# One prefix-product scan over a chunk's four head pairs in place of four, with its factors kept in a tile of their own

## The chip, the cores and the metric

The kernel runs on one core of a Trainium2 chip. The metric is the device time of one execution in microseconds (us). Five engines run their own in-order instruction streams: PE (matrix multiply, with PEld for its weight loads), DVE (elementwise and scans), ACT (activation functions), POOL, and SP, which here only issues transfers. They wait for one another by semaphores.

## The reference, cut to what matters

The program is a gated linear attention, then a two-layer expansion with a squared ReLU, then a soft mixture of experts:

```python
f = 1.0 / (1.0 + np.exp(-f_logit))                      # B=4, H=8, S=768, D=48
for t in range(S):
    state = f[:, :, t, :, None] * state + k_t (outer) v_t
    y[:, :, t] = q_t @ state
x = y as tokens x (heads * D)                           # 3072 x 384
h = np.maximum(x @ w_in, 0.0); x = (h * h) @ w_out      # d_ff = 2048
# then a soft MoE: 8 experts of 4 slots, F = 1024
```

The recurrence is computed by chunks with inverse prefix products: `ip[t]` is the product of `1 + exp(-f_logit)` (that is `1/f`) up to `t`, clamped from above at 1e15. Keys are multiplied by `ip`, queries by `1/ip`, and what remains inside a chunk is a masked matrix product.

## The kernel before, in words

**Attention.** The 3072 tokens are 24 chunks of 128 (`C`), six (`CB`) to a batch row. Eight heads make four pairs (`NP`); a pair lies on 112 partitions (`DD`: head 0 on 0 to 47, head 1 on 64 to 111). `prep(i)` makes a chunk's operands in stages. In the first stage ACT takes `exp(-f)` in place in the chunk's load slot (L154); 1 is added in place, on ACT for the chunks 2, 3 and 4 (`ONACT`, L156) and on DVE for the others (L158); and DVE runs one scan per pair (L160), `state = min(f[t] * state, 1e15)`, whose second operand is one column `big` repeated along 128 elements. A scan begins from 1.0 in a batch row's first chunk (`first`) and otherwise from the last column of the previous chunk's `ip`, read as one value per partition. Chunk 0 is done in two halves of two pairs. In the second stage ACT takes `exp(-ln(ip))` (L167, L168), and DVE makes `kt = k * ip` (L169). In the third stage DVE refines the inverse by a Newton step in a tile `t` with one buffer (L175, L176) and makes `qt = q * -(1/ip)` (L177).

`chunk(i)` is the matrix work: transposes of `kt` (L191) copied by ACT (`n`, L193), scores (L203) masked by DVE (`a`, L206), state updates (L218, added by DVE on L226), and values (L241, L248), which ACT and DVE bring into `y` (L252, L257). `y` is then sent into the token matrix `x` by six small transfers (L263, L266). All transfers are issued by SP in one order: `y` out, the loads of later chunks (`g<-fkq` L134, `v` L136) and the weight loads (`raw<-w` L303). A chunk's `f`, `k` and `q` lie in one of three slots, so a load waits until the last reader (L177) of the chunk three before it is done.

**The expansion.** The tokens are six blocks of 512. For each of the 16 column groups of the hidden layer (`ff`), `layer1` is nine matmuls of 512 columns (L116 to L118, split-precision in three parts), ACT makes `r` and `gh` (L343, L345, L346), DVE makes the remainder `gl` (L348), and `layer2` is nine more matmuls, of which those of L118 need `gl`. Each weight group is loaded raw (L303) and split once: ACT L313, L317 and L111, DVE L318, L319, L327 and L112. A block of `x` is split into two parts (L111 on ACT, L112 on DVE) before its first `layer1`.

**Order.** The program is written as an interleaving (`stream`, `upto`, `target`), and a scheduler that models durations orders each engine's ready instructions, so that neighbours on DVE come from different chunks and from the weight splits. Matrix work of the expansion begins after 23 attention steps (`FIRST`).

Of the kernel before, what the change touches and what calls it, by code (L numbers as in the profile page):

```python
# [7 lines left out]
F32 = mybir.dt.float32  # L8
# [3 lines left out]
AF = mybir.ActivationFunctionType  # L12
ALU = mybir.AluOpType
# [4 lines left out]
NP = H // 2  # L18
HR = 64
DD = HR + D  # L20
TB = 512
NB = B * S // TB
C = 128
# [25 lines left out]
PLACE[6] = [(0, 32, 0, 96), (32, 16, 2, 96)]  # L49
PLACE[7] = [(0, 32, 1, 96), (32, 16, 2, 112)]  # L50
BIG = 1e15
FAR = 1.875 * 2.0**-96
LEAST, MOST = 1.125 * 2.0**-15, 2.0**16 * (1.875 - 2.0**-20)


class K:
# [12 lines left out]

    def consts(self, cp):  # L70
        nc, A = self.nc, self.A
        self.big = cp.tile([DD, 1], F32, name="big")
        nc.vector.memset(self.big, BIG)
        nc.scalar.preload_act_table_set("natural_log_exp_and_others")
        self.mask = cp.tile([128, HC], F32, name="mask")
        self.ident = cp.tile([128, 128], F32, name="ident")
        self.gd = cp.tile([DD, B * NP], F32, name="gd")
        self.ph = cp.tile([128, KT, NS], F32, name="ph")
        self.m = cp.tile([NC * NS, 1], F32, name="m")
        self.wsum = cp.tile([128, NFF], F32, name="wsum")  # L80
        if A["w"].dtype == F32:
            nc.vector.memset(self.wsum, 0.0)
        self.s = cp.tile([NC * NS, 1], F32, name="s")
        self.alpha = cp.tile([NC * NS, 1], F32, name="alpha")
        self.SI = cp.tile([NC * NS, DM], F32, name="SI")
        self.ct = [cp.tile([128, TB], F32R, name=f"ct{b}") for b in range(NB)]
        self.fold = cp.tile([128, 128 + NC], F32, name="fold")
# [11 lines left out]
    def attention_state(self, ap):  # L99

        self.sums = [ap.tile([DD, NP * D + HR - D], F32, name=f"S{j}") for j in range(4)]
        self.turn = 0
        for t in self.sums:
            self.nc.gpsimd.memset(t, 0.0)
# [37 lines left out]
    def prep(self, i):  # L142

        nc, ap = self.nc, self.ap
        U = self.U[i] = {}
        f, k, q, v = self.loaded.pop(i)
        first = i % CB == 0

        parts = [slice(0, NP // 2), slice(NP // 2, NP)] if i == 0 else [slice(0, NP)]
        ip = ap.tile([DD, NP, C], F32, tag="ip", name="ip", bufs=2)  # L150
        kt, qt = (ap.tile([DD, NP, C], F32, tag=n, name=n, bufs=3) for n in ("k", "q"))
        big = self.big.to_broadcast([DD, C])
        for s in parts:
            nc.scalar.activation(f[:, s], f[:, s], AF.Exp, scale=-1.0)  # L154
            if i in ONACT:
                nc.scalar.activation(f[:, s], f[:, s], AF.Copy, bias=1.0)  # L156
            else:
                nc.vector.tensor_scalar(f[:, s], f[:, s], 1.0, None, ALU.add)  # L158
            for p in range(s.start, s.stop):
                nc.vector.tensor_tensor_scan(ip[:, p], f[:, p], big, 1.0 if first else self.ip[:, p, C - 1 : C], ALU.mult, ALU.min)  # L160
        self.ip = ip
        if i % CB == CB - 1:
            bt = i // CB
            nc.vector.tensor_copy(self.gd[:, bt * NP : (bt + 1) * NP], ip[:, :, C - 1])
        yield
        for s in parts:
            nc.scalar.activation(f[:, s], ip[:, s], AF.Ln)  # L167
            nc.scalar.activation(f[:, s], f[:, s], AF.Exp, scale=-1.0)  # L168
            nc.vector.tensor_tensor(kt[:, s], k[:, s], ip[:, s], ALU.mult)  # L169
        U["k"] = kt  # L170
        yield

        t = ap.tile([DD, NP, C], F32, tag="t", name="t", bufs=1)
        for s in parts:
            nc.vector.tensor_tensor(t[:, s], ip[:, s], f[:, s], ALU.mult)  # L175
            nc.vector.scalar_tensor_tensor(t[:, s], t[:, s], 2.0, f[:, s], ALU.subtract, ALU.mult)  # L176
            nc.vector.tensor_tensor(qt[:, s], q[:, s], t[:, s], ALU.mult)  # L177
        yield
        U["v"], U["q"] = v, qt
        yield  # L180
# [604 lines left out]
    def out_of_range(self, pool):  # L785
        nc = self.nc
        bad = pool.tile([128, 1], F32, name="bad")
        nc.vector.tensor_reduce(bad, self.wsum, AX.X, ALU.max)
        nc.vector.tensor_scalar(bad, bad, FAR, None, ALU.is_ge)
        d = pool.tile([DD, 1], F32, name="d")  # L790
        nc.vector.tensor_reduce(d, self.gd, AX.X, ALU.max)
        nc.vector.scalar_tensor_tensor(bad[:DD], d, BIG, bad[:DD], ALU.is_ge, ALU.max)
        row = self.psm()[:1, :128]
# [152 lines left out]
```

## Time and profile before

| what | value |
|---|---|
| median of three runs | 609.6 us (606.76 to 612.16) |
| profiled execution, whole | 605.44 us |
| its span (first to last recorded instruction) | 603.6 us |
| PE busy | 573.8 us (95%) |
| DVE busy | 331.9 us (55%) |
| ACT busy | 316.4 us (52%) |
| mean granted TensorE clock | 0.994 |

The shares are averages over stages that differ: DVE is busy nearly all the time in the first 150 us and about a third of it after 300 us. PE's busy time includes waits inside its pipeline, so a busy PE is not a PE at its peak. The profiled execution is 4.2 us (0.7%) shorter than the median of the runs.

### The profile page before, as it was taken

How to read it: one execution, taken by the hardware profiler on the slowest of the kernel's cores; microseconds unless marked ns; L12 is line 12 of the kernel's file. 1: busy time of each engine (PE TensorE's matmuls, PEld its weight loads, DVE VectorE, ACT ScalarE, POOL GpSimd, SP SyncE). 2: the span in 40 equal slices, each digit the busy share in tenths (PEclk: the TensorE clock that was granted, in tenths of full speed). 3: DMA queues.
4: the chain of work that ended last, by engine and by line, in shares of the span. 5: the costliest groups of instructions: out<-in, count | busy, mean ns of one | idle time of the engine just before them, and what ended most of it. 6: DMA issues, size and time to landing. Idle time of an engine off the chain costs nothing.

```text
span 603.6 us, 13370 instructions
## 1 busy us (share of the span) xinstructions
PE 573.8 (95%) x5611; PEld 447.6 (74%) x5611; DVE 331.9 (55%) x695; ACT 316.4 (52%) x578; POOL 4.0 (1%) x10
## 2 busy tenths in 40 slices
PE   4899989999999999999999999999999999999993
PEld 3786757877777878768778778887788887886372
DVE  6999998999735467455464562542332332213322
ACT  5658778986545456354465353544343544543122
POOL 0000000000000000000000000000000100000000
PEclk9999998999999999999999999999999999999998
DMA  9657778413212202202211211220000735555657
GB/s 292 179 154 200 224 193 309 134 32 82 70 32 68 59 16 73 59 16 73 64 35 50 73 34 46 79 79 3 15 14 3 272 110 168 194 193 174 267 202 272
DMA packets 28324, 69.59 MB, mean 115 GB/s; under 512 B 4464, under 2 KB 17008, under 8 KB 28256
## 3 DMA queue, kind: packets, MB, share of 16 engines
q1 hardware_dynamic: 28256, 68.65, 36.0%
q8 instruction: 46, 0.75, 0.5%
q14 instruction: 22, 0.18, 0.1%
HBM read 59.20 MB, written 4.72 MB: 106 GB/s over the span
## 4 chain that ended last, share of the span: by engine, by line
PE 73%; DVE 9%; DMA 7%; ACT 6%; issue 2%; SPq 1%; ACTq 0%; DVEq 0%
PE o L116 10%; PE ph L116 10%; PE ph L118 9%; PE ph L117 9%; PE o L118 9%; PE o L117 9%; DMA g<-fkq 5%; PE psm L241 3%; DVE ip L160 2%; PE hp L560 2%; PE so L584 2%; PE psm L203 2%; PE psm L218 2%; DMA raw<-w 1%; PE psm L248 1%
## 5 line engine op out<-in xcount | busy, mean ns | idle before, releaser
L348 DVE TENSOR_TENSOR gl<-r,gh 128x512 fp32r<-128x512 f32 x96 | 66.2, 690 | 122.3 <-ACT r L346 121.8
L116 PE MATMUL ph<-x,w 128*128 128x512 f32 x288 | 118.0, 410 | 3.5 <-ACT x L111 2.1
L343 ACT ACTIVATE r<-ph 128x512 f32<-128x512 f32 x96 | 56.9, 593 | 121.5 <-PE ph L118 117.9
L116 PE MATMUL o<-gh,w 128*128 128x512 f32 x288 | 118.0, 410 | 0.0
L118 PE MATMUL ph<-x,w 128*128 128x512 f32 x288 | 113.7, 396 | 0.0
L117 PE MATMUL ph<-x,w 128*128 128x512 f32 x288 | 113.7, 395 | 0.0
L117 PE MATMUL o<-gh,w 128*128 128x512 f32 x288 | 113.1, 393 | 0.0
L118 PE MATMUL o<-gl,w 128*128 128x512 f32 x288 | 111.0, 396 | 1.1 <-DVE gl L348 1.0
L116 PEld LDWEIGHTS ph<-x,w 128*128 128x128 f32 x288 | 54.8, 190 | 19.4 <-issue 4.3
L118 PEld LDWEIGHTS o<-gl,w 128*128 128x128 f32 x288 | 54.0, 188 | 16.3 <-DVE gl L348 5.0
L118 PEld LDWEIGHTS ph<-x,w 128*128 128x128 f32 x288 | 54.5, 190 | 11.9 <-DVE x L112 0.2
L116 PEld LDWEIGHTS o<-gh,w 128*128 128x128 f32 x288 | 54.0, 187 | 12.5
L117 PEld LDWEIGHTS ph<-x,w 128*128 128x128 f32 x288 | 54.9, 191 | 10.9 <-DVE w L112 0.7
L345 ACT ACTIVATE gh<-r 128x512 fp32r<-128x512 f32 x96 | 60.8, 633 | 2.2
L346 ACT ACTIVATE r<-r 128x512 f32<-128x512 f32 x96 | 60.5, 630 | 1.9
L117 PEld LDWEIGHTS o<-gh,w 128*128 128x128 f32 x288 | 54.1, 188 | 9.9
L154 ACT ACTIVATE g<-g 112x512 f32<-112x512 f32 (+1 forms) x25 | 15.2, 611 | 40.2 <-DMA g<-fkq 40.2
L241 PEld LDWEIGHTS psm<-q,S 48*48 48x48 f32 (+1 forms) x704 | 26.5, 143 | 10.4 <-issue 5.6
L160 DVE TENSOR_TENSOR_SCAN ip<-g,ip,big 112x128 f32<-112x128 f32 x80 | 33.8, 469 | 0.6 <-ACT g L156 0.2
L241 PE MATMUL psm<-q,S 48*48 48x64 f32 (+1 forms) x704 | 31.0, 240 | 2.2 <-DVE S L224 1.3
L167 ACT ACTIVATE g<-ip 112x512 f32<-112x512 f32 (+1 forms) x25 | 15.3, 613 | 27.9 <-DVE ip L160 27.7
L177 DVE TENSOR_TENSOR q<-g,t 112x512 f32<-112x512 f32 (+1 forms) x25 | 16.5, 664 | 21.8 <-PE psm L241 21.7
(134 smaller groups left out, 647.1 us busy)
## 6 DMA issues: line engine op xcount, KB each, us to landing
m<-m SPq DMA_DIRECT2D x26, 768.0 KB, 4.3
g<-fkq SPq DMA_DIRECT2D x23, 672.0 KB, 5.3
raw<-w SPq DMA_DIRECT2D x16, 768.0 KB, 5.9
v<-v SPq DMA_DIRECT2D x24, 192.0 KB, 2.9
g<-m SPq DMA_DIRECT2D x6, 768.0 KB, 4.9
out_dram<-ob SPq DMA_DIRECT2D x18, 256.0 KB, 3.4
x<-y SPq DMA_DIRECT2D x48, 72.0 KB, 2.9
x<-y SPq DMA_DIRECT2D x48, 16.0 KB, 1.8
```

The costliest lines, as they stand in the source:

```text
L116: mm(out=out, lhsT=sh, rhs=mh, start=start, stop=False)
L117: mm(out=out, lhsT=sl, rhs=mh, start=False, stop=False)
L118: mm(out=out, lhsT=sh, rhs=ml, start=False, stop=stop)
L154: nc.scalar.activation(f[:, s], f[:, s], AF.Exp, scale=-1.0)
L160: nc.vector.tensor_tensor_scan(ip[:, p], f[:, p], big, 1.0 if first else self.ip[:, p, C - 1 : C], ALU.mult, ALU.min)
L167: nc.scalar.activation(f[:, s], ip[:, s], AF.Ln)
L177: nc.vector.tensor_tensor(qt[:, s], q[:, s], t[:, s], ALU.mult)
L241: nc.tensor.matmul(out=pz[h * HR : h * HR + m, p, r], lhsT=U["S"][c][d, p * D : p * D + m], rhs=U["q"][d, p, r], start=True, stop=True)
L343: nc.scalar.activation(r, o, AF.Relu)
L345: nc.scalar.activation(gh, r, AF.Square)
L346: nc.scalar.activation(r, r, AF.Square)
L348: nc.vector.tensor_tensor(gl, r, gh.bitcast(F32), ALU.subtract)
```

## The change

`consts` loses the column `big`. `attention_state` gets two tiles of 112 x 4 x 129, written once by DVE memsets: `fe` (factors, all 1e20) and `bound` (all 1e15). Column 0 of each pair is the extra one. Per chunk, column 0 of `bound` is set to 1.0 (a batch row's first chunk) or copied from the last column of the previous `ip`; `1 + exp(-f)` is written to columns 1 to 128 of `fe` and no longer in place; and one scan runs over the four pairs laid end to end, 516 elements. At a pair's column 0 the state is multiplied by 1e20 and cut to `bound`, which is the product so far, so the scan restarts there by itself. `ip` becomes a view with a pitch of 129 elements that begins at column 1. The tile `t` is gone: the Newton step writes its values over the factors in `fe`, of which there is one buffer.

```diff
+OVER = 1e20
@@ consts
-        self.big = cp.tile([DD, 1], F32, name="big")
-        nc.vector.memset(self.big, BIG)
@@ attention_state
+        self.fe, self.bound = (ap.tile([DD, NP, C + 1], F32, name=n) for n in ("fe", "bound"))
+        self.nc.vector.memset(self.fe, OVER)
+        self.nc.vector.memset(self.bound, BIG)
@@ prep
-        ip = ap.tile([DD, NP, C], F32, tag="ip", name="ip", bufs=2)
+        ipc = ap.tile([DD, NP, C + 1], F32, tag="ip", name="ip", bufs=2)
+        ip = ipc[:, :, 1:]
+        flat = lambda t, s: t[:, s].rearrange("d p t -> d (p t)")
+        fe, bound = self.fe, self.bound
+        if first:
+            nc.vector.memset(bound[:, :, 0], 1.0)
+        else:
+            nc.vector.tensor_copy(bound[:, :, 0], self.ip[:, :, C - 1])
-        big = self.big.to_broadcast([DD, C])
         for s in parts:
             nc.scalar.activation(f[:, s], f[:, s], AF.Exp, scale=-1.0)
             if i in ONACT:
-                nc.scalar.activation(f[:, s], f[:, s], AF.Copy, bias=1.0)
+                nc.scalar.activation(fe[:, s, 1:], f[:, s], AF.Copy, bias=1.0)
             else:
-                nc.vector.tensor_scalar(f[:, s], f[:, s], 1.0, None, ALU.add)
-            for p in range(s.start, s.stop):
-                nc.vector.tensor_tensor_scan(ip[:, p], f[:, p], big, 1.0 if first else self.ip[:, p, C - 1 : C], ALU.mult, ALU.min)
+                nc.vector.tensor_scalar(fe[:, s, 1:], f[:, s], 1.0, None, ALU.add)
+            nc.vector.tensor_tensor_scan(flat(ipc, s), flat(fe, s), flat(bound, s), 1.0, ALU.mult, ALU.min)
@@ prep, third stage
-        t = ap.tile([DD, NP, C], F32, tag="t", name="t", bufs=1)
+        t = fe[:, :, 1:]
```

## Rows read from the trace of the kernel before

**Rows 1.** Stretches: length, then busy us (instructions) by engine, granted clock, DMA share, GB/s.

```profile
15.00:85.00 70.00, 65.23 (x990) 51.63 (x989) 66.09 (x135) 47.78 (x85) 0.00 (x0) 1.00 0.67 196
85.00:90.00 5.00, 3.06 (x46) 2.00 (x44) 4.60 (x8) 4.01 (x9) 0.00 (x0) 1.00 0.47 99
90.00:95.00 5.00, 4.86 (x17) 3.22 (x18) 5.00 (x8) 3.78 (x7) 0.00 (x0) 0.66 1.00 357
98.00:150.00 52.00, 52.00 (x342) 41.99 (x342) 51.84 (x92) 44.22 (x78) 0.00 (x0) 1.00 0.34 109
98.00:500.00 402.00, 399.67 (x3605) 317.01 (x3605) 215.85 (x441) 216.54 (x397) 2.85 (x2) 1.00 0.22 67
```

**Rows 2.** The chain that ended last, up to 110 us: start, us, what.

```profile
44.54 6.91 DMA g<-fkq
...
63.33 1.52 DVE ip L160 x4
...
78.11 8.66 DMA raw<-w
```

**Rows 3.** The scans, line L160: the first 83 us, then from 98 us on.

```profile
L160 DVE TENSOR_TENSOR_SCAN ip<-g,ip,big x28: 455/462/487, 10.5 to 72.6; 112x128 f32<-112x128 f32 x28
L160 DVE TENSOR_TENSOR_SCAN ip<-g,big x8: 396/406/425, 4.2 to 56.9; 112x128 f32<-112x128 f32 x8
...
L160 DVE TENSOR_TENSOR_SCAN ip<-g,ip,big x52: 457/468/485, 101.6 to 348.3; 112x128 f32<-112x128 f32 x52
L160 DVE TENSOR_TENSOR_SCAN ip<-g,big x8: 400/415/426, 144.2 to 236.9; 112x128 f32<-112x128 f32 x8
```

**Rows 4.** DVE in order of time: start, us, line, what, count [idle before].

```profile
3.86 0.29 DVE L158 TENSOR_SCALAR g<-g 112x256 f32<-112x256 f32 x1 [3.00 <-ACT g L154]
...
10.49 1.60 DVE L160 TENSOR_TENSOR_SCAN ip<-g,ip,big 112x128 f32<-112x128 f32 x4
12.01 0.33 DVE L224 COPY S<-psm 112x192 f32<-112x192 f32 x1
...
47.28 0.16 DVE L164 COPY gd<-ip 112x4 f32<-112x4 f32 x1
47.36 0.69 DVE L169 TENSOR_TENSOR k<-g,ip 112x512 f32<-112x512 f32 x1
...
55.31 0.73 DVE L160 TENSOR_TENSOR_SCAN ip<-g,big 112x128 f32<-112x128 f32 x2
55.96 0.73 DVE L206 TENSOR_TENSOR a<-psm,mask 128x256 f32<-128x256 f32 x2
...
59.91 0.68 DVE L175 TENSOR_TENSOR t<-ip,g 112x512 f32<-112x512 f32 x1
60.51 0.95 DVE L112 TENSOR_TENSOR w<-whi,w 128x768 fp32r<-128x768 f32 x1
```

**Rows 5.** All engines in order of time, around the ACT additions of the chunks 2 and 3.

```profile
13.71 0.61 ACT L156 ACTIVATE g<-g 112x512 f32<-112x512 f32 x1
...
14.23 0.36 ACT L252 ACTIVATE y<-psm 112x256 f32<-112x256 f32 x1
...
15.82 0.67 DVE L177 TENSOR_TENSOR q<-g,t 112x512 f32<-112x512 f32 x1
...
22.12 0.69 DVE L177 TENSOR_TENSOR q<-g,t 112x512 f32<-112x512 f32 x1
22.33 0.63 ACT L156 ACTIVATE g<-g 112x512 f32<-112x512 f32 x1
```

**Rows 6.** PE in order of time, where the second block of tokens begins.

```profile
87.68 0.38 PE L218 MATMUL psm<-v,n 64*48 64x48 f32 x6
90.14 0.50 PE L116 MATMUL ph<-x,w 128*128 128x512 f32 x1 [2.09 <-ACT x L111]
```

**Rows 7.** All engines in order of time, one remainder `gl` and the matmuls that read it.

```profile
103.25 0.68 DVE L348 TENSOR_TENSOR gl<-r,gh 128x512 fp32r<-128x512 f32 x1
...
104.43 0.84 PE L118 MATMUL o<-gl,w 128*128 128x512 f32 x3
```

## The prediction, made before the result was known

> **What bounds the kernel now.** I began with the page's busy shares, but they average over stages, so the view that decides is busy time by stretch [rows 1]. From 98 to 500 us PE is busy for 399.67 of 402 us: whatever DVE does there, only 2.3 us of PE's idle time can be given back. From 15 to 85 us it is DVE that is full, 66.09 of 70 us (94%), while PE's figure of 65.23 us hides short waits between small matmuls. So a shorter DVE instruction can pay only ahead of 98 us, and it pays by letting PE enter its full stretch earlier. Second, the chain of waits [rows 2]: in that early part it goes through scans (63.33 us) but also through transfers of 6.91 and 8.66 us, which no DVE instruction shortens; they move only because SP issues them after a `y` that DVE finished. Third, the scans themselves [rows 3]: 28 + 8 lie in the first 83 us, that is nine chunks (0 to 8), and 52 + 8 after 98 us, fifteen chunks. Fourth, DVE in order of time [rows 4], from which I take prices as distances between starts, because neighbouring instructions overlap: an instruction listed at 0.69 us delays the next by less.
>
> **The scan.** Four scans with an initial value per partition hold DVE from 10.49 to 12.01 us, 1.52 us [rows 4]. Two that begin from the constant hold it from 55.31 to 55.96, 0.65 us, so four take 1.30 us. The long scan of 516 elements stands nowhere in this trace. From above: if a scan's cost were all per element, 0.325 us per 128 makes 1.31 us for 516. From below: an elementwise instruction of 512 delays its neighbour by 60.51 - 59.91 = 0.60 us, and a scan is not likely to be cheaper, so 0.60 us. Between them I need the fixed part of a scan, and take the nearest row of a tiny instruction: the copy of 112x4 at 47.28 delays its successor by 0.08 us. Then an element costs (0.325 - 0.08) / 128 = 1.91 ns and the long scan 0.08 + 516 x 1.91 ns = 1.07 us. I take 1.07.
>
> [...]
>
> **What is added per chunk.** The copy (or the memset to 1.0) of 112x4: 0.08 us as that row, at most the row's whole 0.16 us if the scan must wait for it to finish. So a chunk that is not first saves 1.52 - 1.07 - 0.08 = 0.37 us of DVE, with bounds of 1.52 - 1.31 - 0.16 = 0.05 and 1.52 - 0.60 - 0.08 = 0.84. A first chunk saves 1.30 - 1.07 - 0.08 = 0.15 us (-0.17 to 0.62); chunk 0, in two scans of 258, saves 1.30 - 2 x (0.08 + 258 x 1.91 ns) = 0.15 us as well. Over the nine early chunks: 7 x 0.37 + 2 x 0.15 = 2.9 us; bounds 7 x 0.05 - 2 x 0.17 = 0.0 and 7 x 0.84 + 2 x 0.62 = 7.1 us.
>
> **The two memsets at the start** (112x516 each) cost nothing: DVE sits idle for 3.00 us before its first real instruction at 3.86 us, waiting for ACT and the first load [rows 4]. Even at the elementwise 0.60 us each they are over long before. Without that cover they would add 1.2 us once. The dropped memset of `big` was in the same idle time.
>
> **The factors in one buffer.** `fe` holds the factors of chunk i + 1 and the Newton values of chunk i, so adding 1 for the next chunk waits for L177 of the last. Where DVE adds, this is only DVE's own order: the scan can no longer fill a hole between L175 and L177, but DVE is full anyway. Where ACT adds (chunks 2, 3, 4) it is a new wait across engines, and ACT's stream stands behind it. Chunk 2: L156 ran at 13.71 us, while L177 of chunk 1 ended at 15.82 + 0.67 = 16.49 [rows 5]. Held in place it would hold L252 (14.23 us) and with it the first `y`. The scheduler orders by readiness, so I expect L156 behind those, and the loss is small: chunk 1's scan and Newton step, no longer interrupted by two scans of chunk 2, end about 1 us earlier, and chunk 2's one scan starts later but is shorter. Chunk 3: L156 at 22.33 us against an end of L177 at 22.12 + 0.69 = 22.81: 0.5 us later. I charge 0.5 us, with 0 below, and above it 2.8 + 0.5 = 3.3 us, if L156 of chunk 2 keeps its place.
>
> **The views with a pitch of 129.** L169, L175, L176 and L177 now read or write `ip` and `t` in four runs of 128 at a pitch of 129, L158 writes so. No row of before has an odd pitch. Below nothing is gained; above, the saving of 0.37 us is gone when each of the four grows by 0.09 of its 0.60 us. I take no cost, since the runs stay 128 long and the element counts do not change.
>
> [...]
>
> **The sum.** 2.9 us of DVE time, of which 94% is in a full engine, 2.7 us; less 0.5 us for chunk 3's wait: 2.2 us. After 98 us the same saving of 15 chunks meets a PE that is full, and I count nothing. The profiled execution would go from 605.44 to 603.2 us; that execution is 4.2 us under the median of the runs, and against the median of 609.6 the forecast is 607.4 us. That is 0.4%, less than the 1% that a measurement of this kernel can tell from no change.
>
> **Rivals.**
>
> *It pays nothing (609.6 us).* Either the path ahead of 98 us is set by SP's order and the transfers of 6.91 and 8.66 us, so that DVE's time is taken up by waiting, or the elementwise instructions on odd starts eat the 0.37 us (each 0.09 longer, as above). For the first: transfers make the two longest pieces of the chain there. Against it: DVE is 94% busy, so few of its waits are for transfers.
>
> [...]
>
> *A long scan in front of `gl` (612.6 us, up to 617.8).* From 98 to 150 us DVE is full too, 51.84 of 52 us [rows 1]. There the scans stood singly or in pairs between other work, so that a `gl` waited at most 0.38 us for one. A long scan can't be parted: it holds DVE 1.07 us, 0.69 us longer. `gl` at 103.25 us ended at 103.93, its matmuls began at 104.43, a slack of 0.50 us [rows 7]. Where the scheduler puts a long scan ahead of a ready `gl`, PE loses up to 0.69 us once per chunk: fifteen chunks make 10.4 us at most, half of that 5.2. With the early gain that is 609.6 - 2.2 + 5.2 = 612.6, at most 609.6 - 2.2 + 10.4 = 617.8. It decides from 2.2 / 0.69, some three full hits, on; slower by over 1% takes twelve of fifteen. For it: DVE is in order and full. Against: after 150 us it is not, and the slack covers most of a hit.
>
> **How the numbers follow.** Forecast (607.4) 0.48; nothing 0.22; more than its length 0.16; a long scan before `gl` 0.14. The forecast's own range, from 0.0 and 7.1 us of DVE time and the 0 to 3.3 us on ACT, and from runs that spread over 606.76 to 612.16, is 604 to 611. With half of the third case and most of the fourth the range is 602.5 to 613.5. Faster by over 1% (under 603.5) takes nearly all of the third case or the upper bound of the scan: 0.14. Slower by over 1% (over 615.7) takes nearly the whole of the last one, or the chunk 2 wait in its worst place together with odd starts: 0.06. Within 1%: 0.80.
>
> **What would show it.** In the profile after: one scan per chunk, about 1.07 us from its start to the next instruction's (0.60 or 1.31 would show the step wrong); a tiny copy ahead of it at 0.08; L169 to L177 still at 0.68 to 0.69 us each (0.77 and more would show odd starts); L156 of chunk 2 behind L252; PE's gap of 2.09 us before the second block some 2 us earlier, and the stretch from there on as long as before. The forecast is wrong if the gap does not move, or if matmuls of L118 wait for `gl` more than before.

## The result, and the profile after

The change makes the kernel slower by a small amount: a median of 611.8 us (609.72 to 618.68, 20 runs) against 608.05 us of the kernel before beside it (605.88 to 612.16, 20 runs), a ratio of 1.0065 with an interval of 1.0045 to 1.0084, or +3.9 us by the ratio (the two medians are 3.7 us apart). The forecast was -2.2 us. The result lies within 1% either way, but the sign is wrong, and it is measured.

The profiled execution of the changed kernel takes 613.65 us with a span of 611.9 us, 8.3 us more than that of before. The two are further apart than the medians: before's profile lies 2.6 us under its median, the other 1.9 us above. So I read from them where time goes, and take from the medians how much.

In the code after, the scan is L169, the copy of the bound L161, ACT's addition L166, DVE's L168, and what was L169, L175, L176, L177 is L178, L184, L185, L186; L116 to L118 are L120 to L122, L252 and L255 are L261 and L264, L193 is L202.

Busy time by stretch of the kernel after, columns as in [rows 1]:

```profile
15.00:85.00 70.00, 62.77 (x938) 50.01 (x940) 61.95 (x117) 45.26 (x82) 0.00 (x0) 1.00 0.59 173
85.00:95.00 10.00, 5.72 (x105) 4.30 (x101) 8.12 (x13) 6.76 (x12) 0.00 (x0) 0.92 0.87 280
95.00:100.00 5.00, 4.65 (x11) 3.68 (x12) 4.67 (x7) 3.43 (x6) 0.00 (x0) 0.50 0.91 299
98.00:150.00 52.00, 51.61 (x307) 39.06 (x306) 48.26 (x80) 42.65 (x76) 0.00 (x0) 0.98 0.41 131
```

From 15 to 85 us DVE is now busy 61.95 of 70 us where it was 66.09, and it got through 117 instructions for 135. Four scans became one, so fewer were due; but PE too did only 938 of its 990. DVE did not get done sooner, it waited more. The low clock behind the second block's start is still there, later and longer: 0.50, the lower of the two levels in the clock records of both traces (1.00 and 0.50), from 95 to 100 us costs 5 x 0.50 = 2.5 us, where before lost 5 x 0.34 = 1.7 us [rows 1]; the 0.92 of the ten us ahead of it falls for the most part where PE is idle anyway (93.72 to 95.35 us). (The 1.00 of the first stretch does not hold for all of it; the last section says why.)

DVE in order of time in the kernel after (start, us, line, what, count [idle before]), a chunk's scan and what stands around it:

```profile
0.91 0.49 DVE L104 MEMSET fe<- 112x516 f32 x1 [0.91 <-PEq L948]
1.45 0.49 DVE L105 MEMSET bound<- 112x516 f32 x1
...
4.00 0.30 DVE L168 TENSOR_SCALAR fe<-g 112x256 f32<-112x256 f32 x1 [1.93 <-ACT g L164]
4.33 0.69 DVE L169 TENSOR_TENSOR_SCAN ip<-fe,bound 112x258 f32<-112x258 f32 x1
4.94 0.27 DVE L168 TENSOR_SCALAR fe<-g 112x256 f32<-112x256 f32 x1
...
12.99 0.17 DVE L161 COPY bound<-ip 112x4 f32<-112x4 f32 x1
13.06 0.35 DVE L235 TENSOR_TENSOR S<-S,psm 112x192 f32<-112x192 f32 x1
...
17.04 1.23 DVE L169 TENSOR_TENSOR_SCAN ip<-fe,bound 112x516 f32<-112x516 f32 x1 [0.92 <-ACT fe L166]
...
26.18 1.23 DVE L169 TENSOR_TENSOR_SCAN ip<-fe,bound 112x516 f32<-112x516 f32 x1
27.32 0.40 DVE L215 TENSOR_TENSOR a<-psm,mask 128x256 f32<-128x256 f32 x1
27.63 0.68 DVE L178 TENSOR_TENSOR k<-g,ip 112x512 f32<-112x512 f32 x1
...
34.72 0.96 DVE L116 TENSOR_TENSOR w<-whi,w 128x768 fp32r<-128x768 f32 x1 [1.41 <-ACT w L115]
...
36.26 1.23 DVE L169 TENSOR_TENSOR_SCAN ip<-fe,bound 112x516 f32<-112x516 f32 x1
```

The long scan holds DVE from 26.18 to 27.32 us, 1.14 us; the copy takes 0.07 us to its successor; the memsets end at 1.94 us, ahead of an idle time that still lasts 1.93 us. But chunk 2's scan starts behind 0.92 us of idling, chunk 3's stands at 26.18 us and chunk 4's at 36.26 us. Before, they stood at 22.99 and 32.13 us. This is the same view of the kernel before, where chunk 2's scans run in pieces between chunk 1's Newton steps, with chunks 3 and 4 behind:

```profile
14.44 0.48 DVE L160 TENSOR_TENSOR_SCAN ip<-g,ip,big 112x128 f32<-112x128 f32 x1
14.84 0.67 DVE L176 SCALAR_TENSOR_TENSOR t<-t,g 112x512 f32<-112x512 f32 x1
15.42 0.48 DVE L160 TENSOR_TENSOR_SCAN ip<-g,ip,big 112x128 f32<-112x128 f32 x1
...
22.99 1.61 DVE L160 TENSOR_TENSOR_SCAN ip<-g,ip,big 112x128 f32<-112x128 f32 x4 [0.18 <-ACT g L156]
...
32.13 1.61 DVE L160 TENSOR_TENSOR_SCAN ip<-g,ip,big 112x128 f32<-112x128 f32 x4
```

PE in order of time in the kernel after, first where the first block's 512-column matmuls begin and then where the second block's do:

```profile
49.71 0.80 PE L120 MATMUL ph<-x,w 128*128 128x512 f32 x1 [1.21 <-ACT x L115]
...
92.97 0.75 PE L227 MATMUL psm<-v,n 64*64 64x48 f32 x16 [2.69 <-ACT n L202]
95.35 0.79 PE L120 MATMUL ph<-x,w 128*128 128x512 f32 x1 [1.63 <-ACT x L115]
```

The gap of [rows 6] is not gone and not earlier: the second block's first such matmul moved from 90.14 to 95.35 us.

For all that follows I use five marks of a trace: when the first 512-column matmul starts (A), the 91st (B, where the second block begins), the 169th (C), the 265th (D), and when the last one of the two feed-forward layers starts (E); last, what remains of the span. Times in us, one execution each.

| kernel | A | B | C | D | E | rest |
|---|---|---|---|---|---|---|
| before | 46.70 | 90.14 | 111.00 | 135.21 | 552.35 | 51.25 |
| after | 49.71 | 95.35 | 119.52 | 143.95 | 558.76 | 53.14 |

The 3.0 us lost at A have become 8.5 us at C: 2.2 us are added between A and B and 3.3 between B and C, and some 2.6 of these 5.5 us are clock (2.5 - 1.7 = 0.8 us behind B, some 1.8 us between A and B; last section). From C to E both take about the same, 441.4 and 439.2 us: what was lost ahead of about 120 us is all that is lost there. Another 1.9 us lie behind E and have to do with the clock (last section).

### The profile page after: what moved, and what is told of

The parts are those of the page before. It is cut to its first block, busy times and chain, and to the rows that moved or that the text cites. A ratio compares the mean times of both kernels' runs of the same rounds, so it can differ in the third digit from the quotient of the medians.

```text
span 611.9 us, 13335 instructions
## 1 busy us (share of the span) xinstructions
PE 577.1 (94%) x5611; PEld 449.4 (73%) x5611; DVE 329.2 (54%) x649; ACT 318.3 (52%) x578; POOL 4.0 (1%) x10
## 4 chain that ended last, share of the span: by engine, by line
PE 81%; DMA 5%; DVE 5%; ACT 4%; SPq 2%; issue 2%; ACTq 0%; DVEq 0%
PE ph L120 11%; PE o L120 11%; PE ph L121 10%; PE ph L122 10%; PE o L122 10%; PE o L121 10%; PE psm L250 3%; DMA g<-fkq 3%; DMA raw<-w 2%; PE hp L569 2%; PE psm L212 2%; PE so L593 2%; PE psm L227 2%; PE psm L257 2%; PE psm L393 1%
## 5 line engine op out<-in xcount | busy, mean ns | idle before, releaser
L120 PE MATMUL ph<-x,w 128*128 128x512 f32 x288 | 119.4, 415 | 3.0 <-ACT x L115 2.8
L120 PE MATMUL o<-gh,w 128*128 128x512 f32 x288 | 118.2, 410 | 0.0
L121 PE MATMUL ph<-x,w 128*128 128x512 f32 x288 | 115.1, 400 | 0.0
L122 PE MATMUL ph<-x,w 128*128 128x512 f32 x288 | 114.5, 399 | 0.0
L122 PE MATMUL o<-gl,w 128*128 128x512 f32 x288 | 110.6, 395 | 0.6 <-DVE gl L357 0.5
L120 PEld LDWEIGHTS ph<-x,w 128*128 128x128 f32 x288 | 55.5, 193 | 19.6 <-issue 4.1
L122 PEld LDWEIGHTS ph<-x,w 128*128 128x128 f32 x288 | 55.2, 192 | 12.3
L122 PEld LDWEIGHTS o<-gl,w 128*128 128x128 f32 x288 | 53.7, 188 | 13.9 <-DVE gl L357 2.4
L120 PEld LDWEIGHTS o<-gh,w 128*128 128x128 f32 x288 | 54.0, 187 | 13.1 <-ACT gh L354 0.2
L121 PEld LDWEIGHTS ph<-x,w 128*128 128x128 f32 x288 | 55.6, 193 | 10.6
L186 DVE TENSOR_TENSOR q<-g,fe 112x512 f32<-112x512 f32 (+1 forms) x25 | 16.6, 667 | 26.5 <-PE psm L250 26.4
L169 DVE TENSOR_TENSOR_SCAN ip<-fe,bound 112x516 f32<-112x516 f32 (+1 forms) x25 | 29.6, 1184 | 1.1 <-ACT fe L166 0.9
L176 ACT ACTIVATE g<-ip 112x512 f32<-112x512 f32 (+1 forms) x25 | 15.4, 617 | 28.2 <-DVE ip L169 28.1
L227 PEld LDWEIGHTS psm<-v,n 64*64 64x64 f32 (+1 forms) x704 | 20.7, 145 | 12.1 <-issue 5.9
```

The lines of the kernel that those rows point to most:

```text
L120: mm(out=out, lhsT=sh, rhs=mh, start=start, stop=False)
L121: mm(out=out, lhsT=sl, rhs=mh, start=False, stop=False)
L122: mm(out=out, lhsT=sh, rhs=ml, start=False, stop=stop)
L169: nc.vector.tensor_tensor_scan(flat(ipc, s), flat(fe, s), flat(bound, s), 1.0, ALU.mult, ALU.min)
L227: nc.tensor.matmul(out=pu[c][m, p], lhsT=U["n"][r, p, m], rhs=U["v"][r, hd * D : hd * D + D], start=True, stop=True)
```

## First runs: the shared tile, the loads and the long scan, one at a time

Two other things than the scan had changed in the trace. The factor tile is shared by two chunks, so that ACT's addition for chunk 2 stands behind chunk 1's Newton step. And SP issues chunk 3's load later (SP's DMA issues in order of time, before and then after):

```profile
8.66 0.33 SPq L134 DMA_DIRECT2D g<-fkq  x1
17.63 1.39 SPq L263 DMA_DIRECT2D x<-y  x2
```

```profile
15.60 1.47 SPq L272 DMA_DIRECT2D x<-y  x2
17.12 2.50 SPq L275 DMA_DIRECT2D x<-y  x4
19.66 0.58 SPq L138 DMA_DIRECT2D g<-fkq  x1
```

The first theories were therefore: the single tile costs the time (W), the later load does (L), or the scan that can't be parted does (S). Each got runs.

**e1.** The changed kernel with the Newton step in `q`'s tile.

```diff
-        t = fe[:, :, 1:]
+        t = qt
```

> The changed kernel, but the Newton step works in the chunk's query tile (three buffers) and no longer in the factors' tile; the long scan stays. In its instruction stream SP still issues the load of chunk 3 behind the first y, as in the changed kernel. Theory W (the single factor tile: adding 1 for the next chunk waits for L186 of this one): the wait is gone, 0.31 us per early chunk remain gained, about 606 us, 2 to 3 us under the kernel before, and the first 512-column matmul back at 47 us or sooner. Theory L (the load of chunk 3 issued 11 us later): no change to the changed kernel, 611 to 612 us. Theory S (a long scan can't be parted): 611 to 612 us.

607.0 us, ratio 0.9981 (0.9953 to 1.0008). A is 45.36 us. The loss is gone, with the long scan still in: near what W expected, and against S. It is against L too: SP issues chunk 3's load at 19.46 us here, as late as in the changed kernel.

**e2.** The kernel before with the loads of chunks 3 and 4 issued behind the transfers of `y`.

```diff
+                self.sent = nc.sync.dma_start(out=xl[o : o + n, kt, ts], in_=y[h * HR + e : h * HR + e + n, KT])
...
-                        self.loaded[new] = self.chunk_load(new)
+                        with self.tc.issue_after(self.sent.ins) if new in (3, 4) else ExitStack():
+                            self.loaded[new] = self.chunk_load(new)
```

> The kernel before, with the loads of the chunks 3 and 4 made to follow the six transfers of the y before them on SP, as the changed kernel has it. Theory L: 611 to 612 us, the whole loss of 3.9 us, with the first 512-column matmul near 50 us. Theory W and theory S: 608 us, as the kernel before, since neither the tile nor the scan is changed.

610.2 us, ratio 1.0050 (1.0023 to 1.0077): most of the loss, with none of the change in it.

**e3.** The kernel before, its four scans kept, but the factors written to the tile of the Newton step.

```diff
+        fe = ap.tile([DD, NP, C], F32, tag="t", name="t", bufs=1)
...
-                nc.vector.tensor_scalar(f[:, s], f[:, s], 1.0, None, ALU.add)
+                nc.vector.tensor_scalar(fe[:, s], f[:, s], 1.0, None, ALU.add)
...
-        t = ap.tile([DD, NP, C], F32, tag="t", name="t", bufs=1)
+        t = fe
```

> The kernel before with its four scans, but 1 + exp(-f) is written into the tile t (one buffer) and the Newton step overwrites it there, as the changed kernel does in fe. The load of chunk 3 falls behind the first y here too. Theory W: the loss without the scan's gain, about 3.9 + 2.8 = 6.7 us, 614 to 615 us. Theory L: 611 to 612 us or somewhat more. Theory S: 608 us, since no scan is long.

608.9 us, ratio 1.0016 (0.9999 to 1.0034): about half of the loss at most, with the tile shared and chunk 3's load at 19.44 us. W and L both expected 611 us or more; S, which e1 contradicts, expected 608.

**e4.** The changed kernel with the loads of chunks 3 and 4 issued earlier in the program.

```diff
-                    if j == (4 if i < 2 else 1) and i != 2 and new < NCH:
+                    if j == (0 if i < 2 else 1) and i != 2 and new < NCH:
```

> The changed kernel, with the loads of the chunks 3 and 4 written earlier in the program, so that SP issues the load of chunk 3 ahead of the first y, as in the kernel before. Theory L: 606 to 608 us. Theory W: 611 to 612 us, because the factor tile is still one. Theory S: 611 to 612 us.

604.4 us, ratio 0.9948 (0.9928 to 0.9969). This is faster than both kernels, and faster than any of the theories expected: the change, long scan, shared tile and all, with two loads placed elsewhere.

So far e2 and e4 spoke for L, e1 and e3 against it. The next four crossed the three edits.

**e5.** The same edit of the loads in the kernel before.

> The kernel before, with the same early place of the loads of the chunks 3 and 4 in the program as in the changed kernel with early loads; the load of chunk 3 was ahead of the first y here already, that of chunk 4 moves ahead of the second. If the scan made the gain of 3.1 us in the changed kernel with early loads (theory L: the order of the loads had hidden it), this is 607 to 608 us, as the kernel before. If the edit of the loads itself is what is fast, whatever the scan (rival), this is 604 to 605 us as well.

607.3 us, ratio 0.9978 (0.9953 to 1.0004): the first of its two cases.

**e6.** e1 and e4 together.

> The changed kernel with both repairs: Newton step in the query tile and early loads. If the single factor tile costs something by itself once the loads are early (theory W beside L), 602 to 603 us, 1 to 2 us under the changed kernel with early loads alone. If the tile costs only by way of the late load (theory L alone), 604 to 605 us, the same as with early loads alone.

607.9 us, ratio 0.9990 (0.9967 to 1.0013), neither of its two cases. Taking the shared tile out of e4 does not gain, it loses: against W.

**e7.** e3 with the loads early.

> The kernel before with four scans, the factors and the Newton step in one tile of one buffer, and early loads. Against the changed kernel with early loads (604.4 us) it lacks only the long scan. If the scan's 0.31 us per early chunk is what was gained (2.8 us), 607 us. If the scan's length brings nothing by itself, 604 to 605 us.

611.3 us, ratio 1.0054 (1.0028 to 1.0080), neither of its two cases. The early loads, which gained in e4, go with a loss here: against L.

**e8.** e4 with chunk 3's load early and chunk 4's where it was.

> The changed kernel, with the load of chunk 3 alone written early; that of chunk 4 keeps its late place. Theory L, if it is the load of chunk 3 that counts: 604 to 606 us. If the load of chunk 4 made the gain: 610 to 612 us, as the changed kernel.

610.3 us, ratio 1.0035 (1.0009 to 1.0061): the second of its two cases, as if chunk 4's load had made e4's gain. But e7 loses with both loads early.

Every single theory is contradicted: the same edit gains in one company and loses in another. What all these kernels have in common is that any edit changes the order in which the four instruction streams are laid down when the program is built, everywhere in the first 110 us. That became the next theory (O).

## The order and the instructions, apart

**The means.** The order of each stream can be set by hand: between each instruction and the next of a given list stands a dependency that orders and does not synchronise.

```diff
...
+        for steps in put:
+            at, last = 0, None
+            for step in steps:
+                at += step
+                this = named["I-%d" % at]
+                if last is not None:
+                    tc.add_manual_dep(this, last.name, why, reason="order")
+                last = this
```

`put` holds, for DVE, ACT, SP and PE, the order that another kernel has, its instructions matched one to one by their place in the source, one long scan standing for the four of a chunk (in e10 at the place of the first of them). So a kernel can keep its own instructions, tiles and dependencies in the order of another.

**e9.** The kernel before in the order of the changed kernel.

> The kernel before, every instruction and tile of its own (four scans a chunk, a tile of their own for the Newton step), but each of the DVE, ACT, SP and PE streams is put into the order that the changed kernel has. Theory O (the order of the streams in the first 110 us costs the time, not the instructions): about as slow as the changed kernel, 611.8 us, up to 2.8 us more since the four scans stay: ratio to the kernel before 1.006 to 1.011. Rival T (the long scan or the wait for the shared tile costs the time itself): no change, 608, ratio 0.998 to 1.002.

613.8 us, ratio 1.0074 (1.0046 to 1.0103). The loss is there in full, with four scans, no shared tile, `t` in place and not one instruction of the change. DVE in order of time in e9, the rows that answer to those of the kernel after:

```profile
17.20 1.61 DVE L160 TENSOR_TENSOR_SCAN ip<-g,ip,big 112x128 f32<-112x128 f32 x4 [0.92 <-ACT g L156]
...
26.63 1.60 DVE L160 TENSOR_TENSOR_SCAN ip<-g,ip,big 112x128 f32<-112x128 f32 x4
...
35.54 0.96 DVE L112 TENSOR_TENSOR w<-whi,w 128x768 fp32r<-128x768 f32 x1 [1.41 <-ACT w L111]
...
37.08 1.60 DVE L160 TENSOR_TENSOR_SCAN ip<-g,ip,big 112x128 f32<-112x128 f32 x4
```

The same idle times, 0.92 and 1.41 us, stand at the same places, and chunk 3's scan is as late. They are not waits for the shared tile: L156 writes in place here. ACT in order of time in e9 shows why it is late all the same:

```profile
14.98 0.39 ACT L255 ACTIVATE y<-psm 112x256 f32<-112x256 f32 x1 [0.50 <-PE psm L248]
16.10 0.53 ACT L193 COPY n<-psm 128x448 f32<-128x448 f32 x1 [0.73 <-PE psm L191]
16.53 0.63 ACT L156 ACTIVATE g<-g 112x512 f32<-112x512 f32 x1
```

It stands behind a `y` and an `n` for which ACT waits on PE, by order alone. What e9 does not part is the tile from the order: with one tile chunk 2's factors can be written only behind chunk 1's last Newton step, so a piece of this order is one that the tile demands.

**e10.** The reverse: the long scan (e1's kernel, Newton step in `q`'s tile), its first 1,500 instructions, to beyond the 265th 512-column matmul, in the order of the kernel before.

> The changed kernel with the Newton step in the tile of q (so that the factor tile is free after the scan), its first 1,500 instructions put in the order of the kernel before. Theory O: the time before less what the prediction's prices give for nine chunks, 2.9 us, at most, and 0 at least: 605.2 to 608, ratio 0.995 to 1.000; the first 512-column matmul and the second block's first one not later than 46.7 and 90.1 us. Rival T (the long scan costs by itself, since nothing of a chunk may pass it): 609 or more, ratio over 1.002.

609.35 us, ratio 1.0006 (0.9976 to 1.0036). A is 46.37 and B 91.18 us for before's 46.70 and 90.14. B is 1 us later than expected. In before's order, the long scan costs nothing and gains nothing that can be measured; the end of the range that holds the full 2.9 us (0.995) is excluded, T's 1.002 is not. The scan itself could not be spread as the four were, so some of its saving may have gone there.

**e11.** The changed kernel as it is, shared tile and all, with the first 1,500 instructions of PE, ACT and SP in before's order.

> The changed kernel with its shared factor tile, the first 1,500 instructions of the PE, ACT and SP streams in the order of the kernel before; DVE's order is left free, since before's DVE order is not possible with one tile (chunk 2's scan stands ahead of chunk 1's Newton step there). Theory O: 605 to 608.5, ratio 0.995 to 1.001. Rival W (the wait for the one tile holds DVE and ACT up whatever the order): as the changed kernel, 610 to 614, ratio 1.004 to 1.010.

615.9 us, ratio 1.0120 (1.0083 to 1.0157), worse than the changed kernel. With the shared tile DVE cannot take before's order: there chunk 2's scan begins at 14.44 us, ahead of chunk 1's last Newton step at 15.82 us [rows 5], and with one tile chunk 2's factors may be written only behind that step. Three streams in an order to which the fourth can't keep cost more than an order of their own. Here W's and O's prices are mixed, so it does not say how much the tile alone costs.

**e12.** The kernel before in the order of e4, the fast one.

> The kernel before, all its own instructions and tiles, with all four streams in the order of the changed kernel with its loads issued early (604.4 us, ratio 0.9948). Theory O: most of that gain comes with the order: 604.4 us plus at most 2.8 us for the four scans a chunk: ratio 0.995 to 0.999. Rival T (the gain is the long scan's): 608 or more, ratio 1.000 to 1.005.

606.0 us, ratio 0.9971 (0.9943 to 0.9998). The gain, too, comes with the order, by the middles 1.8 us of e4's 3.2 us; the interval, 0.1 to 3.5 us, leaves the share open. No run sets the kernel before by hand in its own order; but e12, which is faster, and e10 show that the setting by hand does not by itself cost e9's 4.5 us.

The fast order begins like the slow one. DVE in order of time in e4:

```profile
16.86 1.24 DVE L169 TENSOR_TENSOR_SCAN ip<-fe,bound 112x516 f32<-112x516 f32 x1 [0.92 <-ACT fe L166]
...
26.00 1.23 DVE L169 TENSOR_TENSOR_SCAN ip<-fe,bound 112x516 f32<-112x516 f32 x1
...
32.71 1.23 DVE L169 TENSOR_TENSOR_SCAN ip<-fe,bound 112x516 f32<-112x516 f32 x1
```

Chunk 2's scan stands behind the same 0.92 us of idling, and chunk 3's is as late, in a kernel that gains; e12 has the same 0.92 us and chunk 3's scans at 26.70 us. So neither of the two makes a loss by itself. The orders part elsewhere: in e4 chunk 3's load goes out at 8.98 us and chunk 4's at 20.31, in the kernel after at 19.66 and 28.75, and on DVE chunk 4's scan is at 32.71 us in e4 and 33.79 in e12, but at 36.26 in the kernel after and 37.08 in e9.

**What the instructions are worth in one order.** Two pairs now differ by the change alone and share the order. Marks as above:

| kernel | A | B | C | D | E | rest | ratio |
|---|---|---|---|---|---|---|---|
| e9, four scans, order of after | 51.24 | 96.08 | 120.93 | 145.36 | 559.34 | 51.56 | 1.0074 |
| after, long scan | 49.71 | 95.35 | 119.52 | 143.95 | 558.76 | 53.14 | 1.0065 |
| e12, four scans, order of e4 | 50.08 | 91.82 | 112.95 | 138.36 | 552.49 | 53.11 | 0.9971 |
| e4, long scan | 48.34 | 89.72 | 110.63 | 135.99 | 549.75 | 53.05 | 0.9948 |

With the long scan A is earlier by 1.53 and 1.74 us, C by 1.41 and 2.32, D by 1.41 and 2.37, in one execution each. That is about the size that was forecast (2.2 us), and it fits the reason that was forecast, a shorter DVE instruction in the part where DVE is the busiest; the copy and the shared tile, which come with the scan, are not parted from it. In the medians it is 0.0009 and 0.0023 of 608 us, 0.5 and 1.4 us, with intervals that overlap; a median alone would not show it. The order, with the instructions held, is worth +4.5 us (e9) and -1.8 us (e12).

## Which part of the order

What was open then: which streams, and whether the opening or what follows. All four runs are the kernel before with its own instructions.

**e13.** SP alone in the changed kernel's order, and **e14**, DVE, ACT and PE in it and SP in its own.

> The kernel before; SP's stream alone in the changed kernel's order (the load of chunk 3 stands behind the first x<-y transfers), DVE, ACT and PE in their own order. Theory P (the place of the loads costs the time): ratio 1.004 to 1.009, 610.5 to 613.5 us. Theory C (the order of the compute streams costs it): ratio 0.997 to 1.002, 606 to 609 us.

> The kernel before; DVE, ACT and PE in the changed kernel's order, SP in its own (the load of chunk 3 early). Theory P: ratio 0.998 to 1.002, 606.5 to 609 us. Theory C: as e9, ratio 1.005 to 1.010, 611 to 614 us.

634.2 us, ratio 1.0428 (1.0400 to 1.0456), and 621.2 us, ratio 1.0239 (1.0202 to 1.0276). Both expectations fail: neither half carries the loss, each half by itself costs several times the whole. In e13 (DVE's two longest idle times, then SP's issues, then the busy time of a stretch) chunk 3's load goes out at 22.36 us, DVE waits 5.86 us for its factors, and PE's granted clock reads 0.50 (up to 50.6 us that is probably no loss against before; last section):

```profile
28.83 1.61 DVE L160 TENSOR_TENSOR_SCAN ip<-g,ip,big 112x128 f32<-112x128 f32 x4 [5.86 <-ACT g L156]
44.17 0.42 DVE L257 TENSOR_TENSOR y<-y,psm 112x256 f32<-112x256 f32 x1 [6.88 <-ACT y L252]
```

```profile
22.36 0.58 SPq L134 DMA_DIRECT2D g<-fkq  x1
```

```profile
35.00:46.00 11.00, 4.21 (x76) 3.56 (x77) 3.98 (x9) 2.40 (x5) 0.00 (x0) 0.50 0.52 156
```

In e14 the load goes out at 8.78 us, as before, and yet DVE idles 5.60 us ahead of 54.98 us, waiting for ACT's L168. ACT held itself up by order: ahead of that L168 stands a later chunk's L154, which waits 5.16 us, until 53.80 us, for its load. The streams' orders are fitted to each other: the two that cost 1.0428 and 1.0239 apart cost 1.0074 together. So the place of a load is good or bad only with the order of the rest, and that may be why the edits of the loads in e2, e4, e5, e7 and e8 did not add up.

**e15.** The opening in the changed kernel's order (its first 550 instructions, up to the first 512-column matmuls), the rest in before's; and **e16**, the opening in before's order, the rest in the changed kernel's.

> The kernel before; the opening (the first 550 instructions, up to where the 512-column matmuls begin) in the changed kernel's order, all that follows in its own. If the opening costs the time: the first 512-column matmul at 51 us for 46.7 and ratio 1.005 to 1.010, 611 to 614 us. If what follows costs it: ratio 0.998 to 1.002; the late start of the opening is then caught up by the second block's first matmul (90 to 91 us).

> The kernel before; the opening (the first 550 instructions) in its own order, all that follows in the changed kernel's. If the opening costs the time: the first 512-column matmul at 46.7 us and ratio 0.998 to 1.002, 606.5 to 609 us. If what follows costs it: the second block's first matmul at 94 to 96 us all the same and ratio 1.005 to 1.010, 611 to 614 us.

611.2 us, ratio 1.0044 (1.0023 to 1.0066), with A at 51.09 us; and 609.2 us, ratio 1.0015 (0.9995 to 1.0035), with A at 48.83 us. By the middles the opening carries the larger part, 2.7 of the 4.5 us of e9 (its ratio lies just under the expected 1.005); what follows may carry 0.9 us, which is not told from nothing. The two sum to 0.0059 of e9's 0.0074. In e16 A does not come out at 46.7 us as expected: the seam changes the opening's end as well. So it is probably the order ahead of about 50 us that costs most; that halves need not add up, e13 and e14 have shown, and which pair of instructions costs it is not settled.

## Why the prediction was wrong, by its own steps

**What bounds the kernel: right.** Only what happens ahead of PE's full stretch moved the end. From C on, the kernel before takes 441.4 us to E, the kernel after 439.2, e9 438.4, e4 439.1, whatever C was.

**The scan: right, a little low.** 1.07 us was forecast, 1.14 measured (26.18 to 27.32). With chunk 0's scan of 258 at 0.61 us (4.33 to 4.94), an element costs (1.14 - 0.61) / 258 = 2.05 ns and the fixed part is 0.08 us: the fixed part was right, the 1.91 ns per element were 7% low.

**The copy, the memsets, the pitch of 129: right.** The copy costs 0.07 us. The memsets end 1.93 us before anybody is waiting. L178, at 27.63 us, takes 0.68 us as L169 did before, and over the chunks behind chunk 0 the medians of this line, of L184 to L186 and of L168 differ from before by -1 to +7 ns, where the prediction would have lost its gain at 90 ns each: with runs of 128 the odd pitch costs nothing that could be seen here.

**The sum of the instructions: right in size.** By the measured prices a chunk that is not first saves 1.52 - 1.14 - 0.07 = 0.31 us instead of 0.37, nine chunks some 2.3 us instead of 2.9. Within one order A, C and D come 1.4 to 2.4 us earlier.

**The step that failed: the factors in one buffer, and with it the order.** The text says: "The scheduler orders by readiness, so I expect L156 behind those, and the loss is small". The first half held: L166 of chunk 2 runs behind both `y` evictions and an `n` (ACT in order of time, kernel after):

```profile
14.04 0.36 ACT L261 ACTIVATE y<-psm 112x256 f32<-112x256 f32 x1
14.83 0.39 ACT L264 ACTIVATE y<-psm 112x256 f32<-112x256 f32 x1 [0.43 <-PE psm L257]
15.95 0.53 ACT L202 COPY n<-psm 128x448 f32<-128x448 f32 x1 [0.73 <-PE psm L200]
16.38 0.63 ACT L166 ACTIVATE fe<-g 112x512 f32<-112x512 f32 x1
```

The second half did not. The step charged 0.5 us for one wait at chunk 3 and kept every other instruction where it stood. But with the change another order was laid down: chunk 2's scan no longer fills the holes of chunk 1's Newton step, it comes behind 0.92 us of idling, chunk 3's load goes out 11.0 us later (19.66 for 8.66), its scan runs 3.2 us later (26.18 for 22.99) and chunk 4's 4.1 us later. e9 shows that this order costs 4.5 us (2.8 to 6.3 from its interval) without any instruction of the change. The term in the sum that was missing is that; "less 0.5 us for chunk 3's wait" was mis-sized by a factor of about nine, its upper bound of 3.3 us lay below the measured middle, and the sum 2.2 became, with 0.5 to 1.5 us gained and 4.5 lost, a loss. Which of the delays named here carries it is not shown: the idling and the late scan of chunk 3 stand in e4 as well, which gains.

I also named L156 only as a wait of ACT. That chunk 2's short scans were fillers in DVE's holes stood in the trace of before (14.44, 15.42 and 16.40 us), and the text mentions it as harmless, "but DVE is full anyway". Before, the pieces began with no idle time ahead of them; after, the one scan began behind 0.92 us. By e4 that alone did not make the loss.

**The rivals.** "It pays nothing" was nearest. Its mechanism, SP's order and the transfers, is part of it, but e13 and e14 show that no stream's order is the cause alone. "A long scan in front of `gl`" did not happen; the page of the kernel after has for the matmuls that read `gl`:

```profile
L122 PE MATMUL o<-gl,w 128*128 128x512 f32 x288 | 110.6, 395 | 0.6 <-DVE gl L357 0.5
```

0.6 us in all over 288 of them, for 1.1 us before. The gap ahead of the second block neither closed nor moved forward; by the prediction's own test, that "the gap does not move", it was wrong, and the gap moved the other way.

**The range.** 611.8 us lies inside 602.5 to 613.5, and within 1%, but by luck: it is outside the forecast's own 604 to 611 and inside the wider range only for the room that was made for a long scan before `gl`, which did not happen. And the forecast was made against a median of 609.6 us of three runs; against the 608.05 us of twenty, it is a gain of 2.2 us forecast and a loss of 3.9 measured, a miss of 6.1 us. The third case in the range and its 0.16, a gain beyond the forecast's 2.2 us by way of PE's gap ahead of the second block and the low clock behind it, is a term that no run shows: the gap is there in the kernel after, e4, e9 to e12, e15 and e16, with 1.45 us (e12) to 2.85 us (e10), and in e12 the granted clock reads 1.00 from 85 to 110 us in spite of it.

**What stays open.** Why the order that was laid down for the changed kernel is a poor one where e4's, for the same instructions, is a good one, was not settled; nor how much of the order is forced by the shared tile. e1 and e6, without the sharing, and e3, with it, lie between 0.998 and 1.002, so neither forces it one way. Still, of the five kernels that share it and whose streams were not set by hand (after, e3, e4, e7, e8) all but e4 lie above 1.001, and of those that do not (e1, e2, e5, e6) only e2: that the tile disposes to a poor order is a rival that no run rules out. Chunk 4's load is another: it goes out at 28 to 29 us in the kernel after, e2, e8 and e9, which lose, and at 20.3 and 20.6 in e4 and e12, which gain; but e7 loses with it at 21.23, and e3 loses little with it at 30.02.

## What to carry to other kernels

Where the order of the streams is laid down anew with each edit, an edit has two prices: that of its instructions, which can be worked out from rows to a few tenths of a microsecond, and that of the order, here -1.8 to +4.5 us, which the rows of before cannot give. To tell them apart, set the old kernel in the new order and compare; before a small edit is thrown away, move one load or one tile and look whether its gain appears (e4: 0.9948 with the same edit that lost at 1.0065). And short instructions filled holes in a full engine here (14.44 and 15.42 us, between the Newton steps of before): when four become one, look for what they filled, though here the hole that was left cost nothing that could be shown.

## What the runs showed of the hardware that I had not expected

**A clock in the tail with two outcomes.** What follows E takes 51.25 to 51.56 us in seven of the 18 profiled executions and 52.68 to 53.14 us in the other eleven. In all eleven the granted clock drops once while PE still works, across two stretches of 5 us, as here in the kernel after, in and behind a stretch in which PE was idle for 1.3 of 5 us; in all seven it stays at 1.00 until PE's work is over:

```profile
565.00:570.00 5.00, 3.70 (x25) 1.72 (x26) 2.81 (x11) 0.79 (x2) 0.00 (x0) 0.79 0.00 0
570.00:575.00 5.00, 5.00 (x38) 1.41 (x34) 1.38 (x2) 0.73 (x2) 0.00 (x0) 0.87 0.90 317
```

(1 - 0.79) x 5 + (1 - 0.87) x 5 = 1.7 us, and that is about the difference between the two groups. Before had the same idle share there (3.70 of 5 us from 5 us behind E on) and no drop. The group does not go with the change: e9 and the kernel after, in the same order, fall on different sides. So of the 8.3 us between the two profiled spans some 1.7 are this and not the change.

**Matmuls at half speed where the views show a granted clock of 1.00.** In the kernel after, the first block's 512-column matmuls follow each other by 0.43 us; the last two rows are from the stretch with a granted clock of 0.50:

```profile
50.30 0.63 PE L121 MATMUL ph<-x,w 128*128 128x512 f32 x1
50.73 0.63 PE L120 MATMUL ph<-x,w 128*128 128x512 f32 x1
51.16 0.63 PE L122 MATMUL ph<-x,w 128*128 128x512 f32 x1
...
95.94 0.63 PE L121 MATMUL ph<-x,w 128*128 128x512 f32 x1
96.36 0.63 PE L120 MATMUL ph<-x,w 128*128 128x512 f32 x1
```

They do so with interruptions to 59.4 us. In the kernel before the distance is 0.43 us only from 47.3 to 48.6 us, and from 50.6 us on 0.23 us. The views read 1.00 for both, but for this part nothing was measured: the trace holds the granted clock as records, the first of them begins at 59.3 us in the kernel after and at 50.6 us in before, just where the distance changes, and the views show time without a record as 1.00. In these two executions such matmuls in the first 130 us that follow each other directly are 0.23 us apart (median) under a record of 1.00, 0.43 us under a record of 0.50, and 0.43 us, never less, ahead of the first record. So the matmuls that are ahead of the first record ran at the distance of 0.50, and for them the 1.00 from 15 us on in [rows 1] is too high, and so is the mean of 0.994 of before.

Twelve such slow distances in the first block here against three before make some 9 x 0.2 = 1.8 us between A and B; up to 61 us e15, whose opening is in the same order, has six distances of 0.42 or 0.43 us, e12, which gains, has six too, and e10 and e16 have none. So a part of what the order costs, some 1.8 us by these distances, may be paid in clock. What made the clock rise where it did, no run separates.
